# A fused attention and two-layer expert kernel: the last routing of layer one, and layer two's gathers, at other places in the order

## The chip, the cores and the metric

The kernel runs on one core of a Trainium2 chip. The metric is the device time of one execution in microseconds (us); lower is better. The engines are named as in the profile: PE (TensorE), DVE (VectorE), ACT (ScalarE), POOL (GpSimd) and SP (SyncE).

## The reference

Three stages follow one another: a decayed linear attention over 2 x 768 tokens with 8 heads of 64, a layer of 8 experts with one expert for each token, and a layer of 8 experts with two for each token. The last two are what the change touches:

```python
# layer one: N = 1536 tokens, D = 512, E = 8 experts, F = 1024
expert_idx = np.argmax(logits, axis=1)
for e in range(E):
    mask = expert_idx == e
    h = np.maximum(x[mask] @ w1[e], 0.0)
    out[mask] = gate_w[mask, None] * (h @ w2[e])
...
# layer two, on the output of layer one
noisy_logits = logits + noise_scale * noise
top2 = np.argpartition(-noisy_logits, 2, axis=1)[:, :2]
for e in range(E):
    for k in range(2):
        mask = top2[:, k] == e
        h = np.maximum(x[mask] @ w1[e], 0.0)
        out[mask] += top2_w[mask, k, None] * (h @ w2[e])
```

## The kernel before

After the attention, the experts' work is a list of 18 jobs (`JOBS`). Jobs 0 to 7 are layer one's experts, jobs 8 to 17 are layer two's. Jobs 8 and 9 are the first 256 rows of layer two's experts 0 and 1, job 10 is expert 2 with 416 rows; the rest follow. A job has eight steps, one for each block of 128 hidden units (`NF` = 8), and step (j, f) has the number s = 8j + f. The loop at the end of `emit` emits for each step, in this order: `hstep(s)` (the hidden products of this step, 12 matmuls into PSUM tile h, which ACT and DVE split into a high and a low part hs), `ystep(s - 2)` (the output products of the step before the last, into the PSUM tiles y0 to y3), in step (j, 1) `ycopy(j - 1)` (it empties the y tiles of the job before), the weight loads, then the functions that the table `todo` has for (j, f), and last `split(s + 3)` (ACT and DVE make the high and low parts of the weights for three steps later).

The schedule is manual: each engine gets its instructions in the order in which these functions emit them. The h tiles are two, the y tiles one of each. For jobs 8 and 9 `ycopy` calls `put_rows` (L1026 and on): DVE (tile 0) or ACT (tile 1) scales the rows out of y into orow, and POOL scatters them with an accumulating indirect DMA. So the first output product of the next job, in step (j, 2), writes the tile that DVE's orow of the job before reads.

The routing from layer one to layer two goes by job. For job j of layer one, ten stages follow it in later steps: `pe_0`, `pe_1` (logits and rows, on PE and ACT), `post1_a`, `post1_b`, `post1_m`, `post1_h` (noise, the two best experts; small operations of ACT, DVE and POOL), `post1_c`, `post1_c2` (ranks within the experts; c2 also writes job j's rows to the DRAM tensor x2, from POOL), `post1_d` (one-hot tiles pa and pb on DVE) and `post1_e` (four matmuls of pa and pb on PE, and DVE's sum into the table tab2). The tuples `WHEN`, `WHEN5`, `WHEN6` and `WHEN7` say how many steps after the job's end each stage is; a value of 8 is the first step of the job after the next. `WHEN7` is that of job 7, the last of layer one.

Once the table has job 7, layer two's rows can be fetched. `window2(n)` makes indices (g) and validity (ok) from tab2 on DVE; `gather2(j)` has POOL issue an indirect DMA for each 128 rows of job j, from x2 into a tile XW[j]; there are two such tiles. `xmeta(j)` has POOL copy the five last columns of the rows to META[j]; `sel2(j)` has DVE make weights (w) and output row numbers (ix) from META[j], 6 small operations for each pair of tiles; `xprep(j, b)` transposes the rows on PE, and ACT and DVE split them into parts for `hstep`. Steps are set by `put`; the step of window2 and gather2 for jobs 8 to 10 is the last value of the WHEN tuple:

```python
after = {E + i: when[E - 3 + i][-1] % NF for i in range(3)}
for n in range(NEARLY, E + 1):
    put(n + 1, after[n + 2], window2, n)
for j in range(E, NJ):
    put(j - 1, after.get(j, 0), gather2, j)
```

Jobs 9 and 10 have xmeta and sel2 in their own step (j, 0). Job 10's xprep is in (9, 6) and (9, 7). Within one step, before the change, post1_e, pe_0 and pe_1 are sorted to the front, and the others keep the order of their `put`. In the order of `put`, the steps that matter here are: (8, 4): post1_e(6), post1_a(7), window2(7), gather2(9); (8, 5): post1_b(7), post1_m(7); (8, 6): post1_h(7), xprep(9); (8, 7): post1_c(7), post1_c2(7), post1_d(7); (9, 0): xmeta(9), sel2(9); (9, 1), behind ycopy(8): post1_e(7), window2(8), gather2(10), count(1), rank(1); (10, 0): xmeta(10), sel2(10), gather2(11).

Of the kernel before, what the change touches and what calls it, by code (L numbers as in the profile page):

```python
# [58 lines left out]
WHEN = (2, 3, 3, 5, 6, 7, 9, 10, 11, 13)  # L59
WHEN5 = (2, 3, 3, 3, 5, 6, 7, 8, 9, 11)  # L60
WHEN6 = (2, 3, 5, 5, 7, 8, 9, 9, 11, 12)
WHEN7 = (2, 3, 4, 5, 5, 6, 7, 7, 7, 9)
ORDER2 = (0, 1, 2, 5, 3, 6, 4)
XG5 = (5, 6, 6, 4, 5)
XG6 = (6, 6, 6, 8, 8)
# [34 lines left out]
def emit(ctx, tc, kq, kv, lam, moe_expert_emb, moe_tau, moe_w1, moe_w2, moe2_w_gate, moe2_w_noise,  # L100
# [7 lines left out]
    first = moe.enter_context(tc.tile_pool(name="first", bufs=1))  # L108
# [138 lines left out]
    def zero_out(x):  # L247
        r0 = x * 2 * 128
        n = min(2, (OUT_ROWS - r0) // 128)
        if n > 0:  # L250
            nc.scalar.dma_start(dap(out, r0 * DM, [[DM, 128], [128 * DM, n], [1, DM]]),
                              zeros[:, None, :DM].to_broadcast([128, n, DM]))
        if n < 2:
            r0 += n * 128
            nc.scalar.dma_start(out[r0:OUT_ROWS], zeros[:OUT_ROWS - r0, :DM])
# [46 lines left out]
    def wload(u, eng=nc.sync):  # L302
        if u >= 2 * NJ:
            return
        j, half = divmod(u, 2)
        jb = JOBS[j]
        w1, w2 = W[jb.ly]
        if jb.r is None:
            e = jb.e
        elif half:  # L310
            e = EREG[j]
        else:
            drip(99)
            e = nc.values_load(RK[jb.ly][1][0:1, jb.r:jb.r + 1], engines=[eng.engine], min_val=0, max_val=E - 1,
                               skip_runtime_bounds_check_because="a sum of expert numbers times a one-hot row")
            EREG[j] = e
        e = bass.ds(e, 1)
        f0 = half * 512
        r1 = wts.tile([128, KD, 512], FT, name="r1", bufs=RAWB)
        eng.dma_start(r1, w1[e].rearrange("o (k p) f -> p (o k) f", p=128)[:, :, f0:f0 + 512])  # L320
        r2 = wts.tile([128, 4, DM], FT, name="r2", bufs=RAWB)
        eng.dma_start(r2, w2[e].rearrange("o (k p) f -> p (o k) f", p=128)[:, f0 // 128:f0 // 128 + 4])
        RAW[u] = (r1, r2)
# [4 lines left out]
    def drip(n=1):  # L328
        for _ in range(min(n, len(small))):
            fn, *a = small.pop(0)  # L330
            fn(*a)
# [302 lines left out]
    def window_index(ly, tab, g, ok):  # L634

        if ly:
            nc.vector.tensor_scalar(g, tab, -1.0, 0.0, op0=OP.add, op1=OP.max)
        else:
            nc.vector.tensor_copy(g, tab)
        nc.vector.tensor_scalar(ok, tab, 1.0, None, op0=OP.min)  # L640

    def window1(js):
        nc.gpsimd.tensor_mul(ok1[:, js], ok1[:, js], capm[:, js])
        nc.gpsimd.tensor_mul(cid1[:, js], ok1[:, js], sid1.rearrange("p (e t) -> p e t", t=T1)[:, js])
# [10 lines left out]
    def table1():  # L655

        pr = pm.tile([128, 512], FT, name="t", bufs=2)
        for i in JOIN:
            pa, pb = RR[i]
            nc.tensor.matmul(pr[:, :E * NT], pa, pb, start=i == JOIN[0], stop=i == NTI - 1)  # L660
        nc.vector.tensor_add(tab1, tab1, pr[:, :E * NT].rearrange("p (e t) -> p e t", t=NT))
        window_index(0, tab1[:, :S1, :T1], g1[:, :S1], ok1[:, :S1])
        gather(1)
        gather(0)
        window1(slice(0, S1))

    def gather(j, tiles=None, g=None, src=None):
        jb = JOBS[j]
        XW[j] = mo.tile([128, T2 * W2R], FT, name="xw")
        for t in range(jb.nt) if tiles is None else tiles:  # L670
            p = jb.rows(t) if jb.ly else 128
            nc.gpsimd.indirect_dma_start(  # L672
                out=XW[j][:p, t * jb.wr:(t + 1) * jb.wr], out_offset=None, in_=x1[:, :] if src is None else src,
                in_offset=bass.IndirectOffsetOnAxis(ap=(g1[:, j] if g is None else g)[:p, jb.t0 + t:jb.t0 + t + 1],
                                                    axis=0))
# [73 lines left out]
    def hstep(s):  # L749
        j, f = divmod(s, NF)  # L750
        jb = JOBS[j]
        c = jb.c
        h1, l1, _, _ = SPLIT[s]
        ph = pm.tile([128, 512], FT, name="h", bufs=2)
        if l1 is None:
            products(c, [(ph, h1[:, d, :], None, XS[j][1][:, d, :c], d == 0, d == KD - 1) for d in range(KD)])
            hf = mo.tile([128, CR], FT, name="hf", bufs=LAG + 1)
            nc.scalar.activation(hf[:, :c], ph[:, :c], AF.Relu)
            HS[s] = hf[:, :c]
            drip(2)  # L760
            return
        products(c, [(ph, h1[:, d, :], l1[:, d, :], XS[j][0][:, d, :], d == 0, d == KD - 1) for d in range(KD)])
        hs = mo.tile([128, 2 * C2], FR, name="hs", bufs=LAG + 2)
        hh, hl = hs[:, :c], hs[:, c:2 * c]
        HS[s] = hs[:, :2 * c]
        nc.scalar.activation(hh, ph[:, :c], AF.Relu)  # L766
        nc.vector.scalar_tensor_tensor(hl, ph[:, :c], 0.0, hh.bitcast(FT), op0=OP.max, op1=OP.subtract)  # L767
        drip()
# [9 lines left out]
    def ystep(s):  # L778
        j, f = divmod(s, NF)
        if f == 0:  # L780
            PY[j] = [pm.tile([128, 512], FT, name=f"y{d}") for d in range(KD)]
        _, _, h2, l2 = SPLIT[s]
        w = [slice(d * 128, (d + 1) * 128) for d in range(KD)]
        ops = [(PY[j][d], h2[:, w[d]], None if l2 is None else l2[:, w[d]], HS[s],
                f == 0, f == NF - 1) for d in range(KD)]
        if JOBS[j].row:
            last = s >= NSTEP - LAST
            if last and f < NF - 1:
                return
            for t in range(JOBS[j].nt):  # L790
                for x in range(s - LAST + 1 if last else s, s + 1):
                    row_product(x, t)
                if last:
                    put_rows(j, t, PY[j][t], 128)
        else:
            products(JOBS[j].c, ops, not JOBS[j].ly, low_first=True)
        del SPLIT[s], HS[s]

    def ycopy(j):
        jb = JOBS[j]  # L800
        c = jb.c
        if jb.row:
            for t in range(jb.nt):
                put_rows(j, t, PY[j][t], 128)
            return
        yt = yts.rearrange("p (d c) -> p d c", d=KD) if jb.ly else yt1
        YT[j] = yt
        for d in range(KD):
            o = yt[:, d, :c]
            if not jb.ly:  # L810
                nc.scalar.activation(o, PY[j][d][:, c:2 * c], AF.Copy)
                nc.vector.tensor_add(o, PY[j][d][:, :c], o)
            elif d % 2:
                nc.scalar.activation(o, PY[j][d][:, :c], AF.Copy)
            else:
                nc.vector.tensor_copy(o, PY[j][d][:, :c])
# [264 lines left out]
    todo = {}  # L1081
# [92 lines left out]
    stages = (pe_0, pe_1, post1_a, post1_b, post1_m, post1_h, post1_c, post1_c2, post1_d, post1_e)  # L1174
    when = {0: WHEN0, E - 3: WHEN5, E - 2: WHEN6, E - 1: WHEN7}
    after = {E + i: when[E - 3 + i][-1] % NF for i in range(3)}
    for j in range(E):
# [4 lines left out]
        if 0 < j < E - 1:  # L1182
            a = GA if j > 1 else 0
# [33 lines left out]
    for u in range(len(WLOADS), 2 * NJ):  # L1217
        raw = [f % 4 for f in JOBS[(u - 3) // 2].raw if f // 4 == (u - 3) % 2 and u >= 3]
        s = max(0, 4 * (u - 3) + max([WF] + [x + LAG for x in raw]))
        loads.setdefault(s, []).append(u)  # L1220

    table1()
    for s in range(NSTEP + LAG):
        j, f = divmod(s, NF)
        if s < NSTEP:
            hstep(s)

        if s >= LAG and not (f == LAG and 0 < j <= E):
            if f == LAG + 1 and 0 < j <= E:
                ystep(s - LAG - 1)  # L1230
            ystep(s - LAG)
        if f == LAG - 1 and j and not (j == NJ and JOBS[-1].row):
            ycopy(j - 1)
        for u in loads.get(s, ()):
            wload(u, nc.scalar)
        if 12 <= s < 12 + 4 * 8 and s % 4 == 0:
            zero_out(s // 4 - 3)
        for fn, a in sorted(todo.get((j, f), ()), key=lambda x: (post1_e, pe_0, pe_1).index(x[0]) if x[0] in (post1_e, pe_0, pe_1) else 3):
            if fn in stages:
                drip(99)  # L1240
            fn(*a)
        split(s + LEAD)
# [225 lines left out]
```

## Time and profile before

| | |
|---|---|
| median of 3 runs | 597.3 us (596.14 to 597.62) |
| the profiled execution | 597.46 us, of which its span is 595.6 us |
| PE busy | 571.0 us, 96% of the span |
| DVE busy | 376.4 us, 63% |
| ACT busy | 295.1 us, 50% |
| POOL busy | 211.7 us, 36% |
| mean granted clock of TensorE | 0.991 of full speed |

Times in the rows below are microseconds from the start of the span. A row of a timeline has start, duration, engine, line and operation, the tiles written and read, and in brackets how long the engine had been idle before, and what released it. A busy PE is modelled, since matmuls overlap: the next one can start before the end of the one before is shown.

### The profile page before, as it was taken

To read this page: it belongs to the slowest core of one execution; us is meant where nothing else is said; L and a number is where in the kernel's file an instruction comes from. 1 tells how busy PE (TensorE), PEld (TensorE's weight loads), DVE (VectorE), ACT (ScalarE), POOL (GpSimd) and SP (SyncE) were. 2 spreads that over 40 slices of the span, in tenths; PEclk is the share of its full clock that TensorE was granted. 3 is DMA by queue.
4 is the path that set the end of the run, shared out by engine and by line. 5 is a ranking of instruction groups with operands and counts; after the bars stand their busy time and mean duration, and the time that the engine had idled before them with its cause. 6 is when DMAs were issued, how large, how long until landed. Compare 5 with 4: busy or idle time off the path is not lost.

```text
span 595.6 us, 11436 instructions
## 1 busy us (share of the span) xinstructions
PE 571.0 (96%) x4216; PEld 481.4 (81%) x4217; DVE 376.4 (63%) x1162; ACT 295.1 (50%) x696; POOL 211.7 (36%) x408
## 2 busy tenths in 40 slices
PE   5899889999999999999999999999999999999992
PEld 3799779989999899987767888888787898679761
DVE  3588859698898888888867364465663237224620
ACT  3566535776667666675645334344343145314420
POOL 5686544343533523323353201412303342312103
PEclk9899999999999999999999999999999999999997
DMA  6999359768768757856693534446615557747104
GB/s 201 374 295 392 135 162 371 270 225 299 281 230 312 275 178 227 281 170 212 224 316 100 202 142 158 64 174 176 182 55 143 201 114 239 225 144 193 18 6 57
DMA packets 56369, 119.50 MB, mean 201 GB/s; under 512 B 4957, under 2 KB 6533, under 8 KB 56306
## 3 DMA queue, kind: packets, MB, share of 16 engines
q10 hardware_dynamic: 38208, 75.60, 36.6%
q0 software_dynamic: 9376, 25.48, 16.4%
q1 hardware_dynamic: 8722, 17.62, 8.5%
q8 instruction: 35, 0.57, 0.4%
q14 instruction: 28, 0.23, 0.1%
HBM read 100.55 MB, written 18.14 MB: 199 GB/s over the span
## 4 chain that ended last, share of the span: by engine, by line
PE 86%; DMA 5%; DVE 4%; POOL 1%; ACT 1%; issue 1%; SPq 1%; POOLq 0%; DVEq 0%
PE h L730 12%; PE h L731 11%; PE h L735 10%; PE y L728 8%; PE y L735 8%; PE y L730 4%; PE y L731 4%; PE t L711 4%; PE h L741 3%; PE y L741 3%; PE y L775 2%; PE y L776 2%; PE y L774 2%; PE px L432 2%; PE t L1023 2%; PE po L399 2%
## 5 line engine op out<-in xcount | busy, mean ns | idle before, releaser
L730 PE MATMUL h<-xs,h 128*128 128x224 f32 (+10 forms) x512 | 148.9, 314 | 0.0
L731 PE MATMUL h<-xs,h 128*128 128x224 f32 (+10 forms) x512 | 142.4, 302 | 0.0
L1035 POOL DMA_INDIRECT out_dram<-orow,ix x30 | 48.6, 1620 | 206.1 <-DVE orow L1033 151.8
L350 DVE TENSOR_TENSOR l<-r,h 128x512 bf16<-128x512 f32 x128 | 87.9, 687 | 35.0 <-ACT h L348 33.8
L766 ACT ACTIVATE hs<-h 128x224 fp32r<-128x224 f32 (+10 forms) x128 | 51.9, 405 | 103.2 <-PE h L735 102.9
L735 PEld LDWEIGHTS <-l 128*128 128x128 bf16 x896 | 74.0, 97 | 30.6 <-issue 8.2
L731 PEld LDWEIGHTS h<-xs,h 128*128 128x128 f32 x512 | 97.3, 190 | 1.5 <-DVE xs L716 0.5
L730 PEld LDWEIGHTS h<-xs,h 128*128 128x128 f32 x512 | 97.1, 190 | 1.3
L767 DVE SCALAR_TENSOR_TENSOR hs<-h,hs 128x224 fp32r<-128x224 f32 (+10 forms) x128 | 57.8, 452 | 51.1 <-ACT hs L766 50.8
L735 PE MATMUL h<-xs,l 128*128 128x224 bf16 (+10 forms) x512 | 87.4, 291 | 0.0
L352 DVE TENSOR_TENSOR l<-r,h 128x512 bf16<-128x512 f32 x125 | 85.4, 683 | 0.0
L348 ACT ACTIVATE h<-r 128x512 fp32r<-128x512 f32 x128 | 79.8, 623 | 5.7 <-issue 2.2
L349 ACT ACTIVATE h<-r 128x512 fp32r<-128x512 f32 x128 | 79.4, 621 | 0.0
L728 PE MATMUL y<-hs,h 128*128 128x448 f32 (+5 forms) x256 | 64.2, 372 | 0.0
L735 PE MATMUL y<-hs,l 128*128 128x224 bf16 (+8 forms) x384 | 62.5, 284 | 0.0
L716 DVE TENSOR_TENSOR xs<-t,xs 128x416 fp32r<-128x416 f32 (+7 forms) x42 | 24.7, 589 | 54.0 <-ACT xs L715 53.8
L730 PE MATMUL y<-hs,h 128*128 128x416 f32 (+2 forms) x128 | 49.6, 388 | 0.0
L715 ACT ACTIVATE xs<-t 128x416 fp32r<-128x416 f32 (+7 forms) x42 | 21.5, 517 | 53.3 <-PE t L711 50.6
L776 PE MATMUL y<-h,hs 128*128 128x512 f32 x80 | 46.6, 583 | 0.0
L731 PE MATMUL y<-hs,h 128*128 128x416 f32 (+2 forms) x128 | 44.6, 349 | 0.0
L728 PEld LDWEIGHTS y<-hs,h 128*128 128x128 f32 x256 | 42.5, 189 | 0.9
L672 POOL DMA_INDIRECT xw<-x,g x28 | 31.5, 1125 | 18.3 <-PE h L735 7.5
(266 smaller groups left out, 916.6 us busy)
## 6 DMA issues: line engine op xcount, KB each, us to landing
r<-in_moe_w_dram ACTq DMA_DIRECT2D x68, 1024.0 KB, 5.4
kq<-in_kq_dram SPq DMA_DIRECT2D x12, 512.0 KB, 5.8
kv<-in_kv_dram SPq DMA_DIRECT2D x12, 512.0 KB, 6.6
x<-row POOLq DMA_DIRECT2D x8, 517.0 KB, 8.0
r<-in_moe_w_dram SPq DMA_DIRECT2D x4, 1024.0 KB, 9.4
out_dram<-zeros ACTq DMA_DIRECT2D x7, 512.0 KB, 4.8
x<-xr POOLq DMA_DIRECT2D x11, 265.0 KB, 5.1
MT<-zpad SPq DMA_DIRECT2D x2, 256.0 KB, 3.8
```

Source lines behind the costliest of these rows:

```text
L348: nc.scalar.activation(h1, a1, AF.Copy)
L349: nc.scalar.activation(h2, a2, AF.Copy)
L350: nc.vector.tensor_sub(l1, a1, h1.bitcast(FT))
L352: (nc.gpsimd if s < LEAD else nc.vector).tensor_sub(l2, a2, h2.bitcast(FT))
L728: nc.tensor.matmul(o[:, :2 * c], hi, mov, start=first, stop=last, skip_group_check=True)
L730: nc.tensor.matmul(o[:, :c], hi, mov[:, :c], start=first, stop=False, skip_group_check=True)
L731: nc.tensor.matmul(o[:, :c], hi, mov[:, c:], start=False, stop=last, skip_group_check=True)
L735: nc.tensor.matmul(o[:, :c], lo, upper_half(mov[:, :c]), start=first, stop=last, skip_group_check=True)
L766: nc.scalar.activation(hh, ph[:, :c], AF.Relu)
L767: nc.vector.scalar_tensor_tensor(hl, ph[:, :c], 0.0, hh.bitcast(FT), op0=OP.max, op1=OP.subtract)
L776: nc.tensor.matmul(PY[j][t], hl, h2, start=False, stop=f == NF - 1)
L1035: s = nc.gpsimd.indirect_dma_start(out=out[:, :], out_offset=bass.IndirectOffsetOnAxis(ap=ix[:p, t:t + 1], axis=0), in_=row[:p], in_offset ...
```

## The change

The stages a, b, m and h of job 7 go one step earlier each, and the table stage e goes from value 9 to 8, that is from step (9, 1) to (9, 0). With it window2(8) and gather2(10) go to (9, 0), for their step is taken from the same tuple. Then the sorting within a step gets two more names: behind post1_e and ahead of all else come window2 and gather2.

```diff
-WHEN7 = (2, 3, 4, 5, 5, 6, 7, 7, 7, 9)
+WHEN7 = (2, 3, 3, 4, 4, 5, 7, 7, 7, 8)
...
+    first = (post1_e, window2, gather2, pe_0, pe_1)
     table1()
...
-        for fn, a in sorted(todo.get((j, f), ()), key=lambda x: (post1_e, pe_0, pe_1).index(x[0]) if x[0] in (post1_e, pe_0, pe_1) else 3):
+        for fn, a in sorted(todo.get((j, f), ()), key=lambda x: first.index(x[0]) if x[0] in first else len(first)):
```

The steps that differ are then: (7, 3): post1_e(5), window2(6), gather2(8), pe_1(6), where pe_1(6) was second; (8, 3): post1_a(7) joins pe_1(7) and post1_d(6); (8, 4): post1_e(6), window2(7), gather2(9), post1_b(7), post1_m(7); (8, 5): post1_h(7); (8, 6): xprep(9) alone; (9, 0): post1_e(7), window2(8), gather2(10), xmeta(9), sel2(9); (9, 1): count(1), rank(1); (10, 0): gather2(11), xmeta(10), sel2(10). No instruction is added or taken away.

## Rows read from the trace of the kernel before

**Rows 1.** The page: busy us (share of the span) and instructions of each engine.
```profile
PE 571.0 (96%) x4216; PEld 481.4 (81%) x4217; DVE 376.4 (63%) x1162; ACT 295.1 (50%) x696; POOL 211.7 (36%) x408
```
**Rows 2.** Chain of waits that ended last, at 302: start, us, what.
```profile
302.02 6.78 DMA xw<-x,g
```
**Rows 3.** Timeline of PE around the transposes of (9, 6) and (9, 7).
```profile
306.35 0.58 PE L776 MATMUL y<-h,hs 128*128 128x512 f32 x1
307.56 0.30 PE L711 MATMUL t<-ident,xw 128*128 128x128 f32 x1 [0.63 <-DMA xw<-x,g]
...
310.00 0.39 PE L730 MATMUL h<-xs,h 128*128 128x256 f32 x1
...
312.89 1.31 PE L711 MATMUL t<-ident,xw 128*128 128x128 f32 x8
314.14 0.46 PE L730 MATMUL h<-xs,h 128*128 128x416 f32 x1
```
**Rows 4.** Timelines of DVE, POOL and ACT in steps (8, 4) to (8, 6).
```profile
277.00 0.26 DVE L990 TENSOR_TENSOR tab<-tab,t 128x96 f32<-128x96 f32 x1
277.74 1.34 POOL L672 DMA_INDIRECT xw<-x,g  x1 [1.05 <-DVE ok L640]
279.38 0.96 POOL L672 DMA_INDIRECT xw<-x,g  x1 [0.30 <-issue]
282.45 0.20 ACT L935 ACTIVATE q<-q 128x2 f32<-128x2 f32 x1 [0.79 <-POOL q L922]
```
**Rows 5.** Timeline of DVE in steps (8, 7) to (9, 1).
```profile
288.92 0.56 DVE L981 TENSOR_TENSOR pb<-oi,ge 128x384 f16<-128x384 f32 x1
...
290.93 0.15 DVE L1010 SCALAR_TENSOR_TENSOR ws<-meta 128x2 f32<-128x2 f32 x1
...
293.27 0.74 DVE L1033 TENSOR_SCALAR orow<-y,ws 128x512 f32<-128x512 f32 x1
```
**Rows 6.** Timeline of PE: job 9's first output product, in (9, 2).
```profile
294.15 0.47 PE L774 MATMUL y<-h,hs 128*128 128x512 f32 x1
```
**Rows 7.** Timeline of POOL from (8, 7) to (10, 0).
```profile
287.72 0.81 POOL L971 DMA_DIRECT2D x<-row  x1 [0.30 <-POOL row L970]
288.53 0.33 POOL L695 COPY meta<-xw 128x5 f32<-128x5 f32 x2
...
299.26 1.17 POOL L672 DMA_INDIRECT xw<-x,g  x1 [0.30 <-DVE ex L331]
...
303.48 0.89 POOL L672 DMA_INDIRECT xw<-x,g  x1 [0.30 <-issue]
...
313.61 0.87 POOL L672 DMA_INDIRECT xw<-x,g2r  x1 [0.30 <-issue]
314.48 0.09 POOL L1034 MEMSET spacer<- 1x1 f32 x1
```
**Rows 8.** Issue to landing of L971's write: job 7's alone, then all eight.
```profile
DMA to landing us min/median/max: 4.4/4.4/4.4
...
DMA to landing us min/median/max: 3.3/8.0/8.3
```
**Rows 9.** Windows: length, busy us of PE, PEld, DVE, ACT, POOL, granted clock, DMA share, GB/s.
```profile
18.00:18.50 0.50, 0.50 (x10) 0.50 (x8) 0.00 (x0) 0.00 (x0) 0.50 (x1) 0.56 1.02 410
...
21.00:21.50 0.50, 0.50 (x14) 0.50 (x11) 0.00 (x0) 0.50 (x1) 0.50 (x1) 0.53 1.00 393
...
584.00:587.00 3.00, 0.79 (x4) 0.21 (x2) 0.75 (x1) 0.00 (x0) 2.45 (x3) 1.00 0.91 123
588.00:588.50 0.50, 0.00 (x0) 0.00 (x0) 0.00 (x0) 0.00 (x0) 0.00 (x0) 0.58 1.27 131
```
**Rows 10.** Chain of waits, whole span: 16 products of the attention at either clock.
```profile
18.97 1.90 PE po L399 x16
...
24.97 1.02 PE po L399 x16
```
**Rows 11.** Windows, the part of the span behind the change.
```profile
310.00:400.00 90.00, 90.00 (x491) 71.45 (x491) 51.21 (x128) 38.40 (x73) 23.34 (x33) 1.00 0.48 151
```

## The prediction

> **What bounds the kernel now.** I read four views: the page, the chain of waits, and the timelines of each engine around the moved work. TensorE (PE) is busy for 571.0 of 595.6 us [rows 1], so the span changes only by what PE gains or loses. The chain of waits leaves PE in one place that the change touches: for a gather of expert job 10's rows, issued at 302.02 and landed at 308.8 [rows 2]. What the reader is to see on PE's timeline there: the last product of that step starts at 306.35 and ends at 306.93, the transposes of the gathered tile start at 307.56 behind a DMA, and the next step's first matmul at 310.00. In the next step the same eight transposes take 312.89 to 314.14, 1.25 us [rows 3]. Undisturbed they would have ended by 306.93 + 1.25 = 308.2. So the late gather costs PE 310.0 - 308.2 = 1.8 us, a little more since matmuls overlap: I take 1.9. That is all that an earlier gather can give, 0.3% of the time.
>
> **Stages that move (job 7's routing).** No instruction is added or removed; all changes are places in the order. Of the stages of job 7, a, b, m and h go one step up. The first price is on ScalarE. Its small exponential of stage h waits for two POOL operations behind it in data (the last of [rows 4]), and after the change it stands in step (8,5), ahead of ACT's weight copies. POOL has job 9's gathers in front of these two operations, until 279.38 + 0.96 = 280.34 [rows 4]. So ACT waits there until some 281.5 to 282 (an estimate: that end and the two operations), and its later work shifts. Between nothing (the shift is eaten by ACT's idle time) and 1 us of it reaches VectorE's stage d in step (8,7); I take 0.5, the middle, as no row shows it. Stage d's last operation ends at 288.92 + 0.56 = 289.48 now [rows 5], so at about 290.0 after.
>
> **The table at (9,0).** Its four matmuls leave (9,1) and enter (9,0), which costs PE nothing in sum. If PE has to wait there for stage d (until 290.0), this is contained in the longer wait below, since that is counted by absolute times.
>
> **The gathers of job 10 at (9,0).** They need two things. First the indices: VectorE comes to sel2(9), in whose place the table's sum now stands, at 290.93 [rows 5], plus 0.5 for the shift; from the table's sum to the first gather on POOL it took 277.74 - 277.00 = 0.74 us one table earlier [rows 4]; so 290.93 + 0.5 + 0.74 = 292.2. Second, the gathers read the rows of x2 that job 7's own write, issued at 287.72 on POOL [rows 7], puts there. This write landed 4.4 us after its issue; over all eight such writes it was 3.3 to 8.3, median 8.0 [rows 8]. With the 0.5 shift: 287.72 + 0.5 + 4.4 = 292.6, between 291.5 and 296.5. In the kernel before, nothing waited for this write, for the gathers came 11.5 us after it. I take 4.4, because it is the row of the very same write with the same traffic. So the gathers start at 292.6. The Trainium skill (DMA: Bandwidth & Descriptors, "Two DMAs through the same engine are not ordered") says that a DMA reading what an earlier one writes must be held by its issuer until the first one's completion semaphore, even on the same queue. Were there no such wait, the start would be 292.2 and the sum below 0.4 us smaller; no row of before shows either.
>
> **What stands behind them, the main term.** In (9,0) the change puts the gathers ahead of xmeta(9) and sel2(9). On POOL the two small copies of xmeta(9) now stand behind four gathers. POOL works these off in order: a memset that depends on nothing started at 314.48, the moment when the gather in front of it ended (313.61 + 0.87) [rows 7]. The four gathers took from 299.26 to 303.48 + 0.89 = 304.37, 5.1 us, and the two copies 0.33 us [rows 7]. So the copies end at 292.6 + 5.1 + 0.33 = 298.05, where they ended at 288.53 + 0.33 = 288.86.
>
> sel2(9) on VectorE reads these copies. Now it starts at 290.93 without waiting; after the change it starts at 298.1 (0.05 for the hand-over), and everything behind it on VectorE is held: the low weight parts of split(75), the hidden part of step (9,1), and then the scaling of job 8's output rows (orow), which is emitted in ycopy(8). From the start of sel2 to the end of orow it took 290.93 to 293.27 + 0.74 = 294.01, 3.08 us [rows 5]. So orow ends at 301.2. And who waits for that is PE: job 9's first output product goes into the same PSUM tile that orow empties. On the record of before it starts at 294.15, 0.14 us after orow's end [rows 5, 6]; that is already a wait, of a fraction of a us. After the change: 301.2 + 0.14 = 301.3. PE is held 301.3 - 294.15 = 7.15 us later than now, some 6.8 us of it in one idle stretch. PE executes matmuls in order, and the hidden products of the next step stand behind this one, so nothing fills it.
>
> Bounds for this term: without the shift, with the early landing (then the indices decide: 291.7) and with 4.8 us for the gathers (my low estimate, a little under the 5.1) PE resumes at 291.7 + 4.8 + 0.33 + 3.08 + 0.19 = 300.1, so +5.9; with the late landing, 296.5 + 5.1 + 0.33 + 3.08 + 0.19 = 305.2, so +11.0.
>
> **The clock.** At the end PE was busy for only the first 0.79 us of the window 584 to 587, at a granted clock of 1.00 (2.4 GHz), and then idle; in 588.0 to 588.5 the clock was 0.58, so it fell to half (1.2 GHz) there. Near the start it was low from 18.0 to 21.5 (0.56 in the first half microsecond, 0.53 in the last), after a stretch with long waits for loads [rows 9]. In that stretch 16 small products took 1.90 us, and 1.02 at the full clock [rows 10]. An idle stretch of 6.8 us is more than the one at the end needed, so I expect the fall. It costs as much as the low stretch here: 3.45 us of which 3.45 x (1 - 1.02 / 1.90) = 1.6 us are lost. Bounds: 0 if it doesn't fall, 3.2 if it is low for twice as long.
>
> **The other moves.** In (7,3) gather2(8) goes ahead of pe_1(6): POOL then does one small copy behind two gathers, and nobody needs it before stage c2. In (10,0) gather2(11) goes ahead of xmeta(10) and sel2(10): there job 10's rows have landed long before (the third gather took 6.8 us to land [rows 2]), and POOL has been through the gathers of job 11 some microseconds before VectorE comes to sel2(10), so I cost it at nothing; if POOL were late there, up to 5 us. SP's queue holds none of this. ACT's weight load in (9,2) waits for split(75) and so starts about 6 us later, as PE itself does.
>
> **The sum.** +7.15 (PE held at job 9's first output product) - 1.9 (job 10's rows are there at (9,6)) + 1.6 (clock) = +6.85 us. From 310 to 584 PE is busy for the whole of each of three windows, the first of which is shown [rows 11], so no later idle time swallows it. The profiled execution took 597.46 us, 595.6 of it span; the sum on it gives 604.3, on the median of 597.3 it gives 604.1, which I forecast. Its own range is 597.3 + 5.9 - 1.9 + 0 = 601.3 to 597.3 + 11.0 - 1.9 + 3.2 = 609.6.
>
> **The rivals.**
> - *Faster: VectorE is not held.* If the copies of xmeta(9) don't stand behind the gathers, or the gathers hold POOL for no longer than they are handed over, the change only takes away the wait at 307.56: 597.3 - 1.9 = 595.4. It speaks for it that the gather is on the chain of waits; against it, the memset at 314.48. It decides at a delay of sel2(9) by 1.9 us (a start at 292.8), where loss and gain are equal. Chance 0.09.
> - *Nothing to be seen.* POOL gets the copies in behind the first gather: they end at 292.6 + 1.17 + 0.33 = 294.1, sel2 is 3.2 us late, PE as well, less 1.9, with no fall of the clock: 598.6, within 0.3%. The written order speaks against it. Chance 0.06.
> - *The write lands late.* Job 7's rows take 8 us as the median of such writes did: the gathers start at 296.2, 3.6 us later than forecast: 604.1 + 3.6 = 607.7. The slower ACT issues the weight load in front of it, the likelier. Chance 0.13.
> - *Forecast*, 604.1: chance 0.72.
>
> **How the numbers follow.** A measurement of this kernel can tell about 0.3% (1.8 us) from no change. Slower by more than that: 0.72 + 0.13 = 0.85; within: 0.06; faster: 0.09. The range goes from 600.8 (a little under the forecast's lower end, since the copies' place on POOL is argued) to 609.6 and leaves out the two rivals of 0.15 in all.
>
> **What would show it.** Right: POOL's gathers of job 10 start near 292 to 293; the two meta copies behind them; VectorE idle for some 6 to 7 us before the first ws operation, released by POOL meta; PE idle until about 301 before an output product, released by VectorE's orow; a granted clock under 1.00 just behind; and no DMA wait before the transposes of (9,6). Wrong: if the meta copies come before the gathers, or VectorE does orow before sel2, the main term is gone, and the time is 595.4. If PE's idle stretch is there but the clock stays at 1.00, the time is 602.5. If the gathers wait for the write until 296, it is 607.7.

## The result, and the profile after

The changed kernel takes 603.53 us in the median, against 597.27 us of the kernel before on the same chip. It is 6.26 us slower. The ratio measured over the runs is 1.0116, with a 95% interval of 1.0093 to 1.0139; the two medians alone give 1.0105. The forecast was 604.1 us, with +6.85 us.

Its profiled execution took 604.74 us, with a span of 603.0. That is 7.4 us over the span of before, but 1.2 us of it are already there at the first matmul of pe_1(7), in step (8, 3): it starts at 274.18 here, and at 272.99 before. They have nothing to do with the change: the first matmul of the same line in the whole kernel, far ahead of the first step that the change touches, is already 1.14 us late (113.00 against 111.86). 0.8 us of that come from the attention's first loads (PE waits 2.71 us for the second q and k tile, 1.94 before). So all comparisons of traces below use a stretch: from this matmul to the first product of job 10 in (10, 0). It was 314.14 - 272.99 = 41.15 us before and is 321.59 - 274.18 = 47.41 after: +6.26 us, which is the whole loss. Single points are compared after taking off 1.14 us, the lag at the first matmul of post1_c(7) (287.67 against 286.53).

The page of the changed kernel, first part:

```profile
PE 573.5 (95%) x4216; PEld 483.3 (80%) x4217; DVE 375.8 (62%) x1162; ACT 295.2 (49%) x696; POOL 211.6 (35%) x408
```

As many matmuls as in [rows 1], and 2.5 us more of PE's time in them, although no work was added: some of it ran at a lower clock, at the start and in the place that follows.

Timeline of POOL in the changed kernel, from (8, 7) to (9, 1); it answers to [rows 7]:

```profile
288.86 0.81 POOL L971 DMA_DIRECT2D x<-row  x1 [0.30 <-POOL row L970]
293.82 1.04 POOL L672 DMA_INDIRECT xw<-x,g  x1 [4.15 <-DMA x<-row]
...
297.68 0.89 POOL L672 DMA_INDIRECT xw<-x,g  x1 [0.30 <-issue]
298.58 0.32 POOL L695 COPY meta<-xw 128x5 f32<-128x5 f32 x2
```

The write of job 7's rows is issued, POOL waits for its landing, issues four gathers, and only then makes the two copies of xmeta(9), which in [rows 7] followed the write directly.

Timeline of DVE, which answers to [rows 5]:

```profile
290.04 0.56 DVE L981 TENSOR_TENSOR pb<-oi,ge 128x384 f16<-128x384 f32 x1
...
292.42 0.15 DVE L640 TENSOR_SCALAR ok<-tab 128x12 f32<-128x12 f32 x1
298.93 0.16 DVE L1010 SCALAR_TENSOR_TENSOR ws<-meta 128x2 f32<-128x2 f32 x1 [6.35 <-POOL spacer L1034]
...
301.27 0.74 DVE L1033 TENSOR_SCALAR orow<-y,ws 128x512 f32<-128x512 f32 x1
```

DVE has the indices done at 292.57 and then stands for 6.35 us before sel2(9). (The profile names POOL's memset as the releaser; it is the next one behind the copies, which end at 298.90.) And the timeline of PE, which answers to [rows 3, 6]:

```profile
294.78 0.63 PE L735 MATMUL h<-xs,l 128*128 128x256 bf16 x4
302.16 0.76 PE L774 MATMUL y<-h,hs 128*128 128x512 f32 x1 [6.75 <-ACT h L348]
...
304.91 0.37 PE L730 MATMUL h<-xs,h 128*128 128x256 f32 x1
...
316.20 1.31 PE L711 MATMUL t<-ident,xw 128*128 128x128 f32 x8
317.45 0.39 PE L730 MATMUL h<-xs,h 128*128 128x256 f32 x1
```

PE stands for 6.75 us before job 9's first output product, and gets there 302.16 - 1.14 - 294.15 = 6.87 us later than in [rows 6]. The transposes of job 10 in (9, 6) take 1.25 us and wait for nothing: the wait of [rows 3] is gone. The windows of the changed kernel (columns as in [rows 9]) show the clock:

```profile
296.00:298.00 2.00, 0.00 (x0) 0.00 (x0) 0.00 (x0) 0.00 (x0) 1.39 (x3) 1.00 0.68 209
298.00:300.00 2.00, 0.00 (x0) 0.00 (x0) 0.97 (x7) 0.00 (x0) 0.91 (x4) 0.56 0.52 176
...
304.00:305.00 1.00, 1.00 (x4) 0.79 (x4) 1.00 (x3) 0.00 (x0) 0.73 (x3) 0.50 1.05 404
305.00:306.00 1.00, 1.00 (x10) 0.96 (x9) 0.10 (x1) 0.00 (x0) 1.00 (x1) 0.96 1.00 354
```

It falls to half just behind 298, some 3 us into PE's idle stretch, and is back at about 305. From the first output product of (9, 2) to the next step's first hidden product it takes 304.91 - 302.16 = 2.75 us, and 295.62 - 294.15 = 1.47 in the kernel before.

### The profile page after: what moved, and what is told of

It reads as the page before. It is cut to its first block, busy times and chain, and to the rows that moved or that the text cites. A ratio compares the mean times of both kernels' runs of the same rounds, so it can differ in the third digit from the quotient of the medians.

```text
span 603.0 us, 11437 instructions
## 1 busy us (share of the span) xinstructions
PE 573.5 (95%) x4216; PEld 483.3 (80%) x4217; DVE 375.8 (62%) x1162; ACT 295.2 (49%) x696; POOL 211.6 (35%) x408
## 4 chain that ended last, share of the span: by engine, by line
PE 86%; DMA 5%; DVE 3%; POOL 1%; ACT 1%; issue 1%; SPq 1%; POOLq 0%; DVEq 0%; ACTq 0%
PE h L730 12%; PE h L731 11%; PE h L735 10%; PE y L728 8%; PE y L735 8%; PE y L730 4%; PE y L731 4%; PE t L711 4%; PE h L741 3%; PE y L741 3%; PE y L774 3%; PE y L775 3%; PE y L776 3%; DMA xw<-x,g 2%; PE px L432 2%; PE t L1023 2%
## 5 line engine op out<-in xcount | busy, mean ns | idle before, releaser
L348 ACT ACTIVATE h<-r 128x512 fp32r<-128x512 f32 x128 | 79.8, 623 | 10.7 <-DVE hs L767 7.5
L776 PE MATMUL y<-h,hs 128*128 128x512 f32 x80 | 47.5, 593 | 0.0
L774 PE MATMUL y<-h,hs 128*128 128x512 f32 x80 | 35.4, 442 | 6.8 <-ACT h L348 6.8
```

What stands on the lines that cost most here:

```text
L348: nc.scalar.activation(h1, a1, AF.Copy)
L774: nc.tensor.matmul(PY[j][t], hh, h2, start=f == 0, stop=False)
L776: nc.tensor.matmul(PY[j][t], hl, h2, start=False, stop=f == NF - 1)
```

## The experiments

Theory A: in (9, 0) POOL's two small copies stand behind four gathers, VectorE waits for the copies, and PE for what VectorE has behind that wait. Theory B: the price is the gathers' wait for the landing of job 7's rows. Theory C: the price is in the stages a, b, m and h of job 7, which moved up a step. The table has the medians, the ratios over the runs, each against the kernel before on its own chip, and the stretch from (8, 3) to (10, 0) in each profile. On the chips of the experiments the kernel before took 597.64 us (the steps, the sorting, xmeta first, sel2 late), 596.89 us (one gather first, PE kept busy, orow on ACT, stage e alone) and 596.83 us (the last two rows, and the old sorting in (9, 0) alone). The stretch is that of one execution, which lies within 1.9 us of its kernel's median, with one exception: that of one gather first took 604.21 us, 3.5 us over the median, and its nine runs spread from 597.95 to 605.37.

| kernel | median us | ratio, 95% interval | stretch us |
|---|---|---|---|
| before | 597.27 | | 41.15 |
| the change | 603.53 | 1.0116 (1.0093 to 1.0139) | 47.41 |
| only the new sorting | 597.43 | 0.9996 (0.9976 to 1.0016) | 40.98 |
| only the new steps | 603.44 | 1.0107 (1.0086 to 1.0128) | 47.01 |
| the change, old sorting in (9, 0) alone | 595.84 | 0.9974 (0.9952 to 0.9996) | 39.62 |
| the change, xmeta ahead of the gathers | 595.15 | 0.9966 (0.9944 to 0.9988) | 39.51 |
| the change, sel2(9) in (9, 3) | 594.58 | 0.9949 (0.9930 to 0.9968) | 39.10 |
| the change, one gather ahead of xmeta | 600.73 | 1.0061 (1.0031 to 1.0091) | 46.27 |
| the change, PE kept busy | 602.28 | 1.0077 (1.0049 to 1.0105) | 45.82 |
| the change, orow of job 8 on ACT | 602.74 | 1.0104 (1.0067 to 1.0141) | 46.48 |
| xmeta first, stage e alone moved | 595.30 | 0.9972 (0.9955 to 0.9988) | 40.08 |
| before, stage e at value 8 | 595.39 | 0.9983 (0.9968 to 0.9999) | 39.66 |
| the same, sel2(9) in (9, 3) | 594.85 | 0.9978 (0.9958 to 0.9998) | 39.23 |

### The order on POOL alone

```diff
-    first = (post1_e, window2, gather2, pe_0, pe_1)
+    first = (post1_e, xmeta, window2, gather2, pe_0, pe_1)
```

> The changed kernel with one more name in the sorting: xmeta ahead of window2 and gather2. VectorE's own order in (9,0) is that of the changed kernel; only on POOL the two copies go ahead of the gathers. Theory A: 595.8 us, as with the steps alone. Theory B: 603 us, for the gathers wait for the same write. A theory that VectorE's own order (table and indices ahead of sel2) is what costs: 603 us.

595.15 us: the loss is gone and a gain stands in its place. Timelines of POOL and PE of this kernel:

```profile
285.29 0.81 POOL L971 DMA_DIRECT2D x<-row  x1 [0.30 <-POOL row L970]
286.10 0.33 POOL L695 COPY meta<-xw 128x5 f32<-128x5 f32 x2
290.94 1.03 POOL L672 DMA_INDIRECT xw<-x,g  x1 [4.51 <-DVE l L350]
...
292.16 0.47 PE L774 MATMUL y<-h,hs 128*128 128x512 f32 x1 [0.33 <-DVE key L1121]
...
304.77 1.31 PE L711 MATMUL t<-ident,xw 128*128 128x128 f32 x8
```

The copies are done right behind the write's issue; POOL still stands 4.5 us before its first gather, but nobody waits for that; PE stands 0.33 us instead of 6.75, and the transposes still find their rows. VectorE's own order in (9, 0) is that of the changed kernel. So two copies of 0.16 us each, behind the gathers or ahead of them, are worth some 8 us (47.41 against 39.51). Theory B falls: the gathers' wait for the write is in this kernel too. The row names VectorE as the releaser, but the indices were done at 289.02; the write landed 4.9 us after its issue, at 290.2, and the first gather came 0.7 us behind that, as in the changed kernel. (The new name also sorts (10, 0) anew; a kernel below that leaves that step as the change has it loses nothing either.)

### The wait on VectorE taken away instead

```diff
-            put(*((j, 0) if j < E + 3 else (j - 1, 7)), fn, j)
+            put(*((j, 3 if fn is sel2 and j == E + 1 else 0) if j < E + 3 else (j - 1, 7)), fn, j)
```

> The changed kernel with sel2(9) in (9,3) instead of (9,0); xmeta(9) stays behind the gathers on POOL. Theory A: VectorE has nothing to wait for in (9,0), so split, hidden part and orow run on time and PE isn't held; sel2's 0.8 us no longer stand ahead of orow, so the wait of 0.2 us for orow that the kernel before has goes too: 597.3 - 1.9 - 0.2 = 595.2 us. Theories B and C: 603 us. If POOL's scatters behind the gathers hold something else: between.

594.58 us, the lowest median of all. Timelines of PE, POOL and DVE of this kernel:

```profile
292.96 0.48 PE L774 MATMUL y<-h,hs 128*128 128x512 f32 x1
...
296.37 0.32 POOL L695 COPY meta<-xw 128x5 f32<-128x5 f32 x2
...
296.90 0.19 DVE L1010 SCALAR_TENSOR_TENSOR ws<-meta 128x2 f32<-128x2 f32 x1
```

Here the copies still stand behind the gathers; but VectorE reads them only in (9, 3), 0.2 us after they are done, and so orow is on time. The wait of PE before job 9's first output product, 0.33 us in the kernel above, is gone too, since sel2's 0.8 us are no longer ahead of orow. Both ends of the chain have now been cut, each by itself, and either cut is enough.

### Which part of the change does it

Only the new sorting, with the old `WHEN7`:

> Only the new sorting, with the old WHEN7: (9,1) keeps its order, (7,3), (8,4) and (10,0) have the gathers ahead. Theory A: nothing that PE waits for moves, 597.3 us within 0.3%; in (10,0) the copies of xmeta(10) stand behind gather2(11), but VectorE comes to sel2(10) only some 8 us after. If the order in (7,3), (8,4) or (10,0) cost something by itself, the time would be above 599.

597.43 us, no difference, as theory A had it: with the old steps the gathers stand in (9, 1), and no copies are there.

Only the new steps, with the old sorting:

```diff
-    first = (post1_e, window2, gather2, pe_0, pe_1)
+    first = (post1_e, pe_0, pe_1)
```

> Only the new WHEN7, with the old sorting: in (9,0) the order is post1_e, window2, xmeta(9), sel2(9), gather2(10). Theory A (POOL's copies behind the gathers hold VectorE): the copies end near 289 as before, sel2 isn't held, PE's long idle stretch is gone, the gain of 1.9 us at the transposes stays, 0.4 us is lost because the table's sum and the indices now stand ahead of orow on VectorE: 597.3 - 1.9 + 0.4 = 595.8 us. Theory B (the gathers' wait for the landing of job 7's rows is the price) and theory C (the stages a, b, m and h of job 7 going a step up, with ScalarE's wait of 2.1 us for POOL) both have their cause still in this kernel: 603 us.

603.44 us, a miss: I expected 595.8. But the loss lies elsewhere. Timelines of DVE, POOL and PE of this kernel, in (8, 4) to (8, 6):

```profile
275.03 0.24 DVE L990 TENSOR_TENSOR tab<-tab,t 128x96 f32<-128x96 f32 x1
...
277.04 0.15 DVE L637 TENSOR_SCALAR g<-tab 128x2 int32<-128x2 f32 x1
...
277.19 1.31 POOL L921 CAST row<-mi 128x4 f32<-128x4 uint32 x1 [3.88 <-DVE g L637]
...
278.82 1.09 POOL L672 DMA_INDIRECT xw<-x,g  x1 [0.16 <-DVE hs L767]
...
284.88 0.47 PE L711 MATMUL t<-ident,xw 128*128 128x128 f32 x1 [4.38 <-DMA xw<-x,g]
286.61 1.76 PE L711 MATMUL t<-ident,xw 128*128 128x128 f32 x7 [1.26 <-DMA xw<-x,g]
```

Stages b and m now share (8, 4) with the table of job 6, and in the old sorting they stand ahead of window2(7) and gather2(9). The indices come 2.0 us after the table's sum instead of 0.3, the first gather 278.82 - 275.03 = 3.8 us after it instead of 0.74 [rows 4], and PE waits 4.38 + 1.26 = 5.6 us for job 9's rows, most of it at a falling clock (0.76 in the mean of 282 to 284, 0.50 behind). In (9, 2), where the changed kernel loses its time, this kernel's PE stands only 0.34 us, as theory A says. I had read the new sorting as an addition; it is what the new steps need in (8, 4), and what ruins them in (9, 0). The run with the old sorting in that one step separates the two:

```diff
+        names = old if (j, f) == (E + 1, 0) else first
```

> The changed kernel with the old sorting in (9,0) alone, the new one in all other steps. Theory A: the change's loss sits in this one step's order, and the new sorting is needed in (8,4): 595.3 us. If the steps' new places cost by themselves whatever the order, as the run of the steps alone would have it: 603 us.

595.84 us: the loss of the change sits in the order of one step.

Whether the four moved stages are good for anything:

```diff
-WHEN7 = (2, 3, 3, 4, 4, 5, 7, 7, 7, 8)
+WHEN7 = (2, 3, 4, 5, 5, 6, 7, 7, 7, 8)
```

> The kernel with xmeta first, and of the new WHEN7 only the table's value 8; stages a, b, m and h stand where they were before. Theory A: these four moves cost and give nothing: the same time as with xmeta first, 595.8 us by my estimate. Theory C (they cost): faster than that kernel by 0.5 us or more. If the table needs them to be ready at (9,0): slower, with PE waiting for stage d.

595.30 us with xmeta first, against 595.15 with the stages moved: within the intervals no difference. In its profile PE waits 0.24 us for stage d at the table, and 0.27 us for a DMA before job 9's transposes (0.17 in the kernel before). Theory C falls. The smallest version of the change, one number in the kernel before:

```diff
-WHEN7 = (2, 3, 4, 5, 5, 6, 7, 7, 7, 9)
+WHEN7 = (2, 3, 4, 5, 5, 6, 7, 7, 7, 8)
```

> The kernel before with one number changed: the table of job 7 at value 8 (stages a, b, m, h where they were, old sorting). In (9,0) the order is then post1_e, window2, xmeta(9), sel2(9), gather2(10); (8,4) is untouched. Theory A, with what the run of the steps alone added (its loss lay in (8,4), where job 9's indices and gathers had come to stand behind stages b and m): 595.3 us, as with xmeta first. If the loss of that run came from (9,0) after all: 603 us.

595.39 us, ratio 0.9983 (0.9968 to 0.9999, so just clear of no change), with the stretch 1.49 us shorter than before. With sel2(9) in (9, 3) besides:

> The same, and sel2(9) in (9,3), so that VectorE comes to orow 0.8 us earlier and PE's 0.3 us wait before its first output product goes: 594.6 to 595.0 us, the best of the set together with the changed kernel with sel2 late. If VectorE isn't what that product waits for: 595.3 us.

594.85 us, and the stretch 1.92 us shorter. So the table's earlier place does give what the wait at the transposes was worth.

### The dose

The first of job 10's four gathers stays ahead of xmeta(9) and sel2(9); the other three (gather2b, new) are put behind them:

```diff
-        gather(j, range(jb.nt), G2[n, jb.e, jb.r], x2[:n * 256, :])
+        gather(j, range(1 if j == E + 2 else jb.nt), G2[n, jb.e, jb.r], x2[:n * 256, :])
...
+    put(E + 1, 0, gather2b, E + 2)
```

> The changed kernel with only the first of job 10's four gathers ahead of xmeta(9) and sel2(9), the other three behind. Theory A, by dose: the copies end 1.04 + 0.33 us after the first gather's start instead of 4.75 + 0.33, so sel2 and orow come 3.7 us earlier than in the changed kernel and PE's idle stretch is 3.0 us instead of 6.75; whether the clock falls in 3 us is open: 603.5 - 3.7 = 599.8 us with the fall, 598.5 without. Theory B (the wait for the write, which the first gather keeps whole): 603.5 us.

600.73 us: between, but 0.9 over the higher of my two figures. The timelines of POOL and PE (lines behind the edit count one higher) and the windows of this kernel:

```profile
288.44 0.81 POOL L972 DMA_DIRECT2D x<-row  x1 [0.30 <-POOL row L971]
294.34 1.04 POOL L673 DMA_INDIRECT xw<-x,g  x1 [5.09 <-DMA x<-row]
295.37 0.34 POOL L696 COPY meta<-xw 128x5 f32<-128x5 f32 x2
...
299.02 0.76 PE L775 MATMUL y<-h,hs 128*128 128x512 f32 x1 [4.05 <-ACT h L348]
```
```profile
298.00:298.50 0.50, 0.00 (x0) 0.00 (x0) 0.50 (x2) 0.17 (x1) 0.20 (x2) 0.94 0.75 240
298.50:299.00 0.50, 0.00 (x0) 0.01 (x1) 0.50 (x3) 0.50 (x2) 0.50 (x1) 0.50 1.11 231
...
304.50:305.00 0.50, 0.50 (x3) 0.22 (x2) 0.00 (x0) 0.41 (x2) 0.00 (x0) 0.50 0.95 172
305.00:305.50 0.50, 0.50 (x2) 0.36 (x2) 0.49 (x2) 0.50 (x2) 0.00 (x0) 0.73 0.94 221
```

The copies follow the first gather at once, and the stand of PE shrinks from 6.75 to 4.05 us. It would be 3.1, but in this execution the write let the gathers go 294.34 - 288.44 = 5.9 us after its issue, 293.82 - 288.86 = 4.96 in the changed kernel. And the clock, which fell just before PE resumed, stayed low for 6 us of its work. This execution is 3.5 us over its kernel's median, so what the clock cost in it need not be what it costs in the others.

### The clock's share

```diff
+        if s == 8 * (E + 1) + 2:
+            pf = pm.tile([128, 512], FT, name="t", bufs=2)
+            for _ in range(30):
+                nc.tensor.matmul(pf, ones, warm, start=True, stop=True)
```

> The changed kernel with 30 products of constants between hstep and ystep of (9,2), some 6.4 us of PE at full clock into a spare PSUM tile, just where PE idles. If the low clock behind the idle stretch costs 1.3 to 1.6 us, the granted clock stays at 1.00, the first two rows of output products take 1.5 instead of 2.75 us, and the time is 603.5 - 1.3 = 602.2 us. If the clock costs nothing of its own: 603.5 us.

602.28 us, as expected. Windows and PE's timeline of this kernel:

```profile
298.00:300.00 2.00, 2.00 (x11) 0.88 (x9) 1.97 (x6) 0.12 (x1) 0.00 (x0) 1.00 0.14 45
...
300.57 0.47 PE L774 MATMUL y<-h,hs 128*128 128x512 f32 x1 [0.20 <-ACT h L348]
```

PE does 30 useless products, the clock stays at 1.00, and the output product starts as late as in the changed kernel (300.57 - 286.16 = 14.41 us behind post1_c(7)'s first matmul; 302.16 - 287.67 = 14.49 there). The stretch is 47.41 - 45.82 = 1.6 us shorter. That is the price of the clock by itself; the medians are 1.25 us apart, which agrees with it, but their two intervals overlap.

### What PE waits for

The profile names ACT's weight copy (L348) as the releaser of PE's long stand, not orow.

```diff
-        if t % 2:
+        if t % 2 or j == E:
```

> The changed kernel with both orow tiles of job 8 scaled by ScalarE, so that PE's first output product doesn't need VectorE. Theory A: the output products run at about 295.3 of the changed kernel's timeline instead of 302.16; then PE is held at the hidden products of (9,3), whose PSUM tile VectorE's hidden part of (9,1) must empty (it ends at 301.4): 603.5 - 3.4 = 600.1 us without a fall of the clock, up to 601.8 with one. If PE waits for ScalarE's weight copy instead, which the profile names as the releaser: 603.5 us.

602.74 us. PE's timeline of this kernel:

```profile
292.89 0.48 PE L774 MATMUL y<-h,hs 128*128 128x512 f32 x1
...
299.86 0.58 PE L730 MATMUL h<-xs,h 128*128 128x256 f32 x1 [5.32 <-DVE hs L767]
```

With orow on ScalarE the output products of (9, 2) run at once, while ACT's weight copy comes at 299.93, as late as ever: so PE hadn't waited for that copy, but for VectorE's orow, which ended at 302.01 in the changed kernel, 0.15 us ahead of PE's start (0.14 before). Then PE stands all the same, 5.32 us, before the hidden products of (9, 3), whose PSUM tile VectorE's hidden part must empty first. I expected a gain of 1.7 to 3.4 us; it was 0.8 by the medians, which the intervals don't tell from nothing, and 0.9 by the stretch. PE resumes into the low clock and works at it from 299.86 to about 303.5, 3.7 us against 2.9 in the changed kernel. Besides, in this execution the write let the gathers go 292.29 - 286.61 = 5.7 us after its issue, 4.96 in the changed kernel: that is 0.7 us more of standing, about what the stretch lacks to the lower end of my range.

## Why the prediction was right

**What bounds, and what there was to gain.** The wait at the transposes was taken as 1.9 us. In the changed kernel it is gone: from the start of the last output product ahead of the transposes of (9, 6) to the first product behind them it takes 317.45 - 315.78 = 1.67 us there and 310.00 - 306.35 = 3.65 before, 1.98 us less. The six kernels without the loss have a stretch 1.1 to 2.05 us shorter; the two above 1.9 have sel2 late and so also save PE's short wait for orow. Right.

**Stages that move.** I had 0.5 us of shift for stage d. ACT did wait for POOL, 2.11 us, but stage d's last operation ended at 290.60, less the 1.14 of lag 289.46, against 289.48 before [rows 5]: no shift at all. The term was mis-sized, and the row to take would have been ACT's idle time behind it.

**The gathers' start.** 292.6 was forecast; it was 293.82 - 1.14 = 292.68. That it came out so close is luck, for errors cancel: no shift of 0.5, a landing 0.2 us sooner, but 0.7 us from the landing (4.21 us after 288.86, at 293.07) to the first gather, which I had left out. That the gathers wait for the write is what the row says: 4.15 us of POOL's idle time put down to DMA x<-row. The indices were done at 292.57, 1.25 us ahead of the first gather. The Trainium skill (DMA: Bandwidth & Descriptors, "Two DMAs through the same engine are not ordered") asks for this wait, and the trace agrees. The landing took 4.2 us, near the 4.4 of the same write, and not the 8.0 of the median; the rival of a late landing did not come, though the run with one gather first had a touch of it.

**The main term.** Four gathers 5.1 us forecast, 298.57 - 293.82 = 4.75 measured; from sel2's start to orow's end 3.08 forecast, 301.27 + 0.74 - 298.93 = 3.08 measured; PE at the output product +7.15 forecast, +6.87 measured. That it is this chain and no other is shown at both ends: by the copies taken ahead, and by sel2 taken away.

**The clock.** 1.6 us forecast, and 1.6 us by the kernel that keeps PE busy; by the terms it is 6.31 - 6.87 + 1.98 = 1.4 (with the stretch from post1_c(7), 33.92 - 27.61 = 6.31, and the transposes' gain as 1.98). The fall was argued from rows and came; its size is in part luck. I had taken the length of the low stretch at the start, 3.45 us. Here the clock was low for 2.9 us of PE's work, but for 3.7 with orow on ScalarE and for some 6 in the execution with one gather first.

**The rivals.** "VectorE is not held" is the kernel with sel2 late: 594.58, forecast as 595.4 for its case. So the time of this rival was about right; its condition did not hold. That POOL gets the copies in between the gathers is what the kernel with one gather first does by its order; POOL itself never took them out of order. My price for it, 598.6, was too low (600.73); I had let the clock stay up, and in the one trace of it the clock fell.

**The other moves.** I cost gather2(8) in (7, 3), gather2(9) in (8, 4) and gather2(11) in (10, 0) at nothing. For the sorting alone that is right (597.43). But I did not see that in (8, 4) the new sorting pays for something: without it the new steps lose 5.9 us in sum, by the stretch. The sum did not need it; an engineer who had undone only the sorting would have.

## What to carry to other kernels

An operation that is moved ahead on one engine delays everything that it passes there; list what it passes, and for each of these who waits for it and what stands behind that waiter in its queue. Here the place of two copies of 0.16 us decided over some 8 us, across three engines. Before a gather goes ahead of small work on the same queue, put that small work first, or move its reader to where nobody waits.

## What was not expected of the hardware

The price of the low clock did not follow the length of the idle stretch. After 6.75 us of standing PE resumed about 3 us before the clock came back, and lost 1.4 us. After 4.05 us, with one gather first, the clock fell half a microsecond before PE resumed, was low for some 6 us of its work, and the loss by the same terms was 32.70 - 27.61 - 4.15 + 1.98 = 2.9 us. That was an execution 3.5 us over its kernel's median; by the medians, with the wait and the gain of that trace, the loss would be 600.73 - 596.89 - 4.15 + 1.98 = 1.7 us, an estimate. After 5.32 us, with orow on ScalarE, PE worked 3.7 us at the low clock. So what a stall costs beyond itself is open by one to two us until the trace is there. Why the low stretch is longer in one execution than in another, no run here shows.
